# Two accumulators of one tile read by VectorE at a block's end, and a buffer of its own for the last block's gate product

## The chip, the cores and the metric

The program runs on one core of a Trainium2 chip. The metric is device time in microseconds (us), the median of several executions. The core has five engines with an instruction queue each: TensorE (PE in the profile; PEld are its weight loads), VectorE (DVE), ScalarE (ACT), GpSimd (POOL) and SyncE (SP), which here only issues transfers. TensorE adds its products up in the accumulation memory (PSUM); the other tiles lie in the on-chip memory (SBUF).

## The reference

Attention of two kinds on 4 x 8 heads of 576 positions, then two layers on the 2304 tokens. The change lies in the first layer and at its hand-over to the second.

```python
x = attention(q, k, v)            # pooled by 4, plus local |i - j| < 4
x = x.transpose(0, 2, 1, 3).reshape(2304, 512)
a = x @ w_a                       # 512 -> 1536, the gate
b = x @ w_b                       # 512 -> 1536
y = a * b @ w_out                 # 1536 -> 512, the first layer's result

h = y @ w_in                      # 512 -> 1024
e = exp(h - max(h)); sm = e / (sum(e) + 1e-9)
s = h * sm
ln = (s - mean(s)) / sqrt(var(s) + 1e-6) * g_ln
out = ln @ w_out2                 # 1024 -> 512
```

## The kernel before, in words

Every fp32 operand is split into a high and a low part, and each product is made of three matmuls (high x high, high x low, low x high).

**First layer.** The tokens go through in five blocks: four of 512 columns (`WIDE`) and a last one of 256. A block runs over 12 chunks `j` of the 1536 inner columns. For a chunk, `emit_A` with n=0 makes the gate product and with n=1 the second one (12 matmuls each, into `ab`, of which there are two tiles). `emit_a` copies the gate product out of PSUM (ScalarE, L478, tile `a`), `emit_mult` multiplies it by the second product (VectorE, L483), `emit_p` splits the result into `ph` (ScalarE, L489) and `pl` (GpSimd, L490), and `emit_B` adds the chunk into four accumulators (L507, 3 matmuls each, m = 0 to 3). Tile `a` has one buffer: the copy of chunk j+1 must wait until `pl` of chunk j, its last reader, is made. In a block of 512 columns two of the accumulators are tiles of their own (`acc0`, `acc1`); the other two are halves of one tile, `accS`. In the last block of 256 columns the gate and the second product of a chunk share one `ab` tile, and the four accumulators share two tiles. Waits are kept by tile: a matmul into one half of `accS` waits for a read of its other half.

**A block's end.** `emit_B` of chunk 11 copies each accumulator out as soon as its own three matmuls are issued (ScalarE, L514, tile `o`) and stores it to DRAM (`o1d`, L515, SP). It is called one chunk late, between the products of the next block; next come 32 small matmuls of local attention (`lS`, L353) and the gate product of the next block's chunk 1.

**Beside the last block** the second layer starts. Its 16 weight pieces are loaded (`raw`, L101, 512 KB each) into the places of first-layer weights that the last block is done with, so each load waits for a product of that block. ScalarE (L109, L110, L123 or L125) and VectorE (L114, L117, L130 or L132; four pieces use GpSimd for the last step) turn a piece into its two parts. The first layer's results come back (`o1r`, L530) and are split (L536, L537), and the products `h` (L548, 24 matmuls for each of 18 token tiles) begin. Then for each tile: maximum, exponential, mean (L557 to L577), a transpose through DRAM, and the product `o` (L616).

**The order** of instructions comes from a scheduler that plays the program through with its own cost estimates. `pin` holds TensorE's order as written through the first four blocks (all engines in the first). In the last block and after, the scheduler orders every engine, TensorE too.

Of the kernel before, what the change touches and what calls it, by code (L numbers as in the profile page):

```python
# [7 lines left out]
F32 = mybir.dt.float32  # L8
# [15 lines left out]
WIDE = 512  # L24
# [3 lines left out]
NCH = FF1 // 128  # L28
# [10 lines left out]
def kernel(  # L39
# [17 lines left out]
    PE, ACT, DVE, POOL, SP = nc.tensor, nc.scalar, nc.vector, nc.gpsimd, nc.sync  # L57
# [17 lines left out]
    base = pool("base", bufs=1)  # L75
# [7 lines left out]
    width = [min(WIDE, NT - WIDE * i) for i in range(NBLK)]  # L83
    o1d = [dram.tile([w // 128, 128, 512], F32, name=f"o1d{i}") for i, w in enumerate(width)]
# [371 lines left out]
    accs = {}  # L456
    abs_ = {}
    o1s = {}
# [15 lines left out]
                          start=(k == 0 and i == 0), stop=(k == 3 and i == 2), skip_group_check=True)  # L474

    def emit_a(blk, j):
        a = base.tile([128, WIDE], F32, tag="a", name="a")[:, 0:width[blk]]
        ACT.copy(out=a, in_=abs_[blk, j][0])  # L478
        abs_[blk, j].append(a)

# [12 lines left out]
    def emit_B(blk, j):  # L493
        w = width[blk]
        if j == 0:
            if w == WIDE:
                t = aps.tile([128, 2, 512], F32, tag="S", name="accS")
                accs[blk] = [ps.tile([128, 512], F32, tag=f"acc{n}", name=f"acc{n}") for n in range(2)] + [t[:, n] for n in range(2)]
            else:
                t = [ps.tile([128, 2, 256], F32, tag=f"acc{n}", name=f"acc{n}") for n in range(2)]  # L500
                accs[blk] = [t[n // 2][:, n % 2, :] for n in range(4)]
        ph, pl = pt.pop((blk, j))
        wh, wl = W1[3 * j + 2]
        for m in range(4):
            ms = slice(m * 128, m * 128 + 128)
            for i, (wt, x) in enumerate(((wh, ph), (wh, pl), (wl, ph))):
                PE.matmul(out=accs[blk][m], lhsT=wt[:, ms], rhs=x,  # L507
                          start=(j == 0 and i == 0 and (w == WIDE or m % 2 == 0)), stop=(j == NCH - 1 and i == 2),
                          skip_group_check=True)
            if j == NCH - 1:  # L510
                if m == 0:
                    o1s[blk] = base.tile([128, NP, WIDE], F32, tag="xs", name="o1")
                o1 = o1s[blk][:, m, 0:w]
                ACT.copy(out=o1, in_=accs[blk][m])  # L514
                SP.dma_start(out=o1d[blk][:, :, 128 * m:128 * m + 128].rearrange("i p t -> p i t"),  # L515
                              in_=o1.rearrange("p (i t) -> p i t", t=128))


    p2 = {}
# [170 lines left out]
    for i in range(6, 3 * NCH):  # L690
        j = i // 3
        t = 4 * j - 6 + 1.33 * (i % 3)
# [38 lines left out]
    for blk in range(NBLK - 1):  # L731
        for j in range(NCH):
            c = NCH * blk + j
            if c == 4:
                SP.dma_start(out=g_sb, in_=g)
            if c:
                emit_A(blk, j, 0, 0, WIDE)
            emit_a(blk, j)
            if c:
                advance(4 * c + 1.33)  # L740
                emit_A(blk, j, 1, 0, WIDE)
            emit_mult(blk, j)
            if j == NCH - 1:
                advance(4 * c + 2)
                emit_p(blk, j)
                split_x(blk + 1)
                advance(4 * c + 2.67)
            else:
                advance(4 * c + 2.67)
                emit_p(blk, j)  # L750
            if prev:
                emit_B(*prev.pop())
            prev.append((blk, j))
            advance(4 * c + 4)
            pin(None if blk == 0 else (PE.engine,))
    blk = NBLK - 1
    advance(1e9)
    for j in range(NCH):
        if j == 2:
            start_p2()  # L760
        for n in range(2):
            emit_A(blk, j, n, 0, width[blk])
            (emit_mult if n else emit_a)(blk, j)
        emit_p(blk, j)
        prev.append((blk, j))
        if len(prev) > 2 or j < 1:
            emit_B(*prev.pop(0))
        if j == 8:
            split_o1(0)
            split_o1(1)  # L770
            load_o1(2)
            load_o1(3)
        for t_, f in w2q:
            if t_ == j:
                f()
    for x in prev:
        emit_B(*x)
# [92 lines left out]
```

## Time and profile before

| | |
|---|---|
| median of 3 executions | 805.21 us (800.87 to 806.71) |
| the profiled execution | 803.08 us, of which the span from the first to the last instruction is 801.3 us |
| TensorE busy in the span | 765.4 us (96%), mean granted clock 0.988 |
| VectorE, ScalarE, GpSimd busy | 376.9, 332.5, 228.5 us |

A matmul's time in the profile reaches from its start to the modelled end, and matmuls overlap, so the distance between two starts is the pace. An idle time stands in square brackets with the engine and line that ended it. Times in the trace count from the first instruction; what lies outside the span is 803.08 - 801.3 = 1.8 us.

### The profile page before, as it was taken

The page shows a single profiled execution, that of the slowest core. Times are in us where ns is not written, and L with a number is a line of the kernel's source. Part 1 is how long each engine was busy: PE and PEld are TensorE (multiplying, and loading weights), DVE is VectorE, ACT ScalarE, POOL GpSimd, SP SyncE. Part 2 cuts the span into 40 slices and gives each one's busy share as a digit, 9 for nine tenths or more (in the row PEclk, how much of TensorE's full clock was granted, in tenths as well). Part 3 has the DMA queues.
Part 4 walks back from the last instruction along what each step waited for, and adds up shares of the span by engine and source line. Part 5 has one row for each costly group of instructions (what it writes and reads, how often), then busy time and mean ns, then how long its engine had stood idle before and what let it go on. Part 6 is the DMA issues. An engine that isn't in the chain of part 4 may idle for free.

```text
span 801.3 us, 12378 instructions
## 1 busy us (share of the span) xinstructions
PE 765.4 (96%) x4848; PEld 621.3 (78%) x4848; DVE 376.9 (47%) x689; ACT 332.5 (41%) x691; POOL 228.5 (29%) x204
## 2 busy tenths in 40 slices
PE   4979999998999999999999999999899999999997
PEld 3867777776787787777787888888788888888885
DVE  5678889974223324223213220126765373545441
ACT  3648777653222324322323221147645343344432
POOL 1242343431322222232111121114222352334320
PEclk9979999999999999999999999999999999999999
DMA  8977844214212203111102000036422554444321
GB/s 239 239 259 246 268 152 137 70 30 139 59 57 61 83 30 110 59 52 34 42 15 80 15 27 1 0 112 208 155 79 66 157 173 144 145 134 145 103 79 40
DMA packets 65226, 85.04 MB, mean 106 GB/s; under 512 B 9016, under 2 KB 46136, under 8 KB 65168
## 3 DMA queue, kind: packets, MB, share of 16 engines
q1 hardware_dynamic: 64864, 84.02, 33.8%
q8 instruction: 38, 0.62, 0.3%
q10 hardware_dynamic: 304, 0.23, 0.1%
q14 instruction: 20, 0.16, 0.1%
HBM read 66.93 MB, written 17.30 MB: 105 GB/s over the span
## 4 chain that ended last, share of the span: by engine, by line
PE 81%; DVE 7%; ACT 5%; DMA 3%; issue 3%; POOL 1%; SPq 0%; DVEq 0%; ACTq 0%; POOLq 0%
PE ab L473 33%; PE o L616 13%; PE h L548 11%; PE acc L507 8%; PE accS L507 7%; PE lo L412 2%; PE pv L283 2%; PE lPT L393 2%; DVE wm L117 2%; DMA qkr<-qkp 1%; PE lS L353 1%; PE S L223 1%; DMA raw<-w 1%; PE PT L266 1%; ACT o L514 1%
## 5 line engine op out<-in xcount | busy, mean ns | idle before, releaser
L473 PE MATMUL ab<-xTh,w 128*128 128x512 f32 (+1 forms) x976 | 298.0, 375 | 6.2 <-DVE a L483 3.6
L473 PEld LDWEIGHTS ab<-xTh,w 128*128 128x128 f32 x976 | 179.9, 191 | 43.7 <-DVE a L483 5.6
L473 PE MATMUL ab<-xTl,w 128*128 128x512 f32 (+1 forms) x488 | 180.2, 369 | 0.9 <-DVE xTl L167 0.5
L490 POOL TENSOR_TENSOR pl<-a,ph 128x512 fp32r<-128x512 f32 (+1 forms) x60 | 75.1, 1251 | 234.6 <-ACT ph L489 234.6
L483 DVE TENSOR_TENSOR a<-a,ab 128x512 f32<-128x512 f32 (+1 forms) x60 | 38.0, 632 | 181.3 <-PE ab L473 181.3
L473 PEld LDWEIGHTS ab<-xTl,w 128*128 128x128 f32 x488 | 93.4, 191 | 15.1 <-DVE xTl L167 0.9
L548 PE MATMUL h<-w,o1w 128*128 128x512 f32 x432 | 103.9, 391 | 1.1 <-ACT w L123 0.9
L548 PEld LDWEIGHTS h<-w,o1w 128*128 128x128 f32 x432 | 80.1, 188 | 18.1 <-ACT w L123 1.1
L616 PE MATMUL o<-w,cTh 128*128 128x512 f32 x288 | 91.0, 397 | 1.2 <-ACT cTh L606 0.9
L507 PE MATMUL acc<-ph,w 128*128 128x512 f32 (+1 forms) x288 | 90.2, 365 | 0.0
L478 ACT COPY a<-ab 128x512 f32<-128x512 f32 (+1 forms) x60 | 32.5, 542 | 108.9 <-PE ab L473 103.7
L507 PE MATMUL accS<-ph,w 128*128 128x512 f32 x192 | 68.0, 391 | 4.2 <-ACT o L514 4.2
L616 PEld LDWEIGHTS o<-w,cTh 128*128 128x128 f32 x288 | 54.0, 188 | 14.3 <-ACT cTh L606 1.1
L489 ACT CAST ph<-a 128x512 fp32r<-128x512 f32 (+1 forms) x60 | 34.6, 577 | 67.2 <-DVE a L483 67.2
L507 PEld LDWEIGHTS acc<-ph,w 128*128 128x128 f32 x288 | 52.2, 189 | 9.1 <-issue 1.2
L616 PE MATMUL o<-w,cTl 128*128 128x512 f32 x144 | 57.2, 397 | 0.1
L507 PE MATMUL acc<-pl,w 128*128 128x512 f32 (+1 forms) x144 | 51.1, 358 | 0.1
L600 POOL TENSOR_TENSOR cTl<-raw,cTh 128x1024 fp32r<-128x1024 f32 x15 | 36.0, 2401 | 44.2 <-ACT cTh L599 36.6
L507 PEld LDWEIGHTS accS<-ph,w 128*128 128x128 f32 x192 | 36.0, 188 | 13.1 <-ACT o L514 5.5
L117 DVE CUSTOM_DVE_ANT_0 wm<-raw,wm 128x1024 uint16<-128x1024 uint16 x52 | 43.4, 845 | 2.3
L255 POOL TENSOR_TENSOR E<-E,ss 72x576 f32<-72x576 f32 x16 | 19.3, 1206 | 81.1 <-DVE ss L253 53.4
L557 DVE TENSOR_REDUCE mx<-h 128x1 f32<-128x1024 f32 x18 | 22.0, 1223 | 43.1 <-PE h L548 43.1
(91 smaller groups left out, 1005.5 us busy)
## 6 DMA issues: line engine op xcount, KB each, us to landing
raw<-w SPq DMA_DIRECT2D x52, 512.0 KB
qkr<-qkp SPq DMA_DIRECT2D x32, 288.0 KB
vd<-v SPq DMA_DIRECT2D x15, 512.0 KB
raw<-vd SPq DMA_DIRECT2D x60, 128.0 KB
vw<-vwin SPq DMA_DIRECT2D x36, 140.0 KB
vp<-vp SPq DMA_DIRECT2D x16, 288.0 KB
o1r<-o1d SPq DMA_DIRECT2D x18, 256.0 KB
out<-ob SPq DMA_DIRECT2D x18, 256.0 KB
```

The source lines that it names most:

```text
L117: DVE.tensor_tensor(out=st["w"], in0=st["w"], in1=st["low"], op=ALU.add)
L255: POOL.tensor_tensor(out=ev, in0=ev, in1=st["ss"].to_broadcast([72, 4, SD]), op=ALU.mult)
L473: PE.matmul(out=abs_[blk, j][n][:, c0:c1], lhsT=w[:, ws], rhs=x[:, k, c0:c1], start=(k == 0 and i == 0), stop=(k == 3 and i == 2), skip_gr ...
L478: ACT.copy(out=a, in_=abs_[blk, j][0])
L483: DVE.tensor_tensor(out=a, in0=a, in1=pb, op=ALU.mult)
L489: ACT.copy(out=ph, in_=a)
L490: POOL.tensor_tensor(out=pl, in0=a, in1=f32(ph), op=ALU.subtract)
L507: PE.matmul(out=accs[blk][m], lhsT=wt[:, ms], rhs=x, start=(j == 0 and i == 0 and (w == WIDE or m % 2 == 0)), stop=(j == NCH - 1 and i == ...
L548: PE.matmul(out=h[:, n * 512:n * 512 + 512], lhsT=x[:, ks], rhs=w, start=(k == 0 and q_ == 0), stop=(k == 3 and q_ == 2))
L557: DVE.tensor_reduce(out=mx, in_=st["h"], axis=AX.X, op=ALU.max)
L600: POOL.tensor_tensor(out=h4(lo), in0=raw, in1=f32(h4(hi)), op=ALU.subtract)
L616: PE.matmul(out=o, lhsT=x[:, k, :], rhs=w, start=(k == 0 and q_ == 0), stop=(k == 7 and q_ == 2))
```

## The change

In a 512-column block the copies for m = 0 and 1 stay where they are, on ScalarE. The copies for m = 2 and 3, the two halves of `accS`, move behind the last matmul of the block and from ScalarE to VectorE, and their two stores with them. In the last block the gate copy gets a tag `a2` of its own with two buffers of 256 columns.

```diff
     def emit_a(blk, j):
-        a = base.tile([128, WIDE], F32, tag="a", name="a")[:, 0:width[blk]]
+        if width[blk] == WIDE:
+            a = base.tile([128, WIDE], F32, tag="a", name="a")
+        else:
+            a = base.tile([128, 256], F32, tag="a2", bufs=2, name="a")
         ACT.copy(out=a, in_=abs_[blk, j][0])
...
+        def store(m):
+            SP.dma_start(out=o1d[blk][:, :, 128 * m:128 * m + 128].rearrange("i p t -> p i t"),
+                         in_=o1s[blk][:, m, 0:w].rearrange("p (i t) -> p i t", t=128))
...
-                o1 = o1s[blk][:, m, 0:w]
-                ACT.copy(out=o1, in_=accs[blk][m])
-                SP.dma_start(out=o1d[blk][:, :, 128 * m:128 * m + 128].rearrange("i p t -> p i t"),
-                              in_=o1.rearrange("p (i t) -> p i t", t=128))
+                if m < 2 or w < WIDE:
+                    ACT.copy(out=o1s[blk][:, m, 0:w], in_=accs[blk][m])
+                    store(m)
+        if j == NCH - 1 and w == WIDE:
+            for m in (2, 3):
+                DVE.tensor_copy(out=o1s[blk][:, m, 0:w], in_=accs[blk][m])
+                store(m)
```

Through the first four blocks the order on TensorE and GpSimd stays as it was; ScalarE loses and VectorE gains two copies at each block's end. There ScalarE has, before, at the end of the first block (`o` is the copied result, `lP` and `E` belong to attention):

```order
L514 COPY o_2079<-acc_885 128x512
L489 CAST ph<-a 128x512
L514 COPY o_2079<-acc_886 128x512
L514 COPY o_2079<-accS 128x512 x2
L374 ACTIVATE lP<-lP 128x560
```

The two `accS` copies now stand on VectorE at the same place, between the multiplication of the next block's chunk 0 and the mask of the local attention (`lP`), with the multiplication of chunk 1 further behind:

```order
L486 TENSOR_TENSOR a<-a,ab 128x512
L253 RECIPROCAL ss<-ss 72x4
L526 COPY o_2079<-accS 128x512 x2
L364 TENSOR_TENSOR lP<-lS,mk_sb 128x280 x2
L370 TENSOR_REDUCE lmx<-lP 128x8
L371 TENSOR_TENSOR lP<-lP,lmx 128x560
L380 TENSOR_REDUCE lsm<-lP 128x8
L381 TENSOR_SCALAR lsm<-lsm 128x8
L382 RECIPROCAL lsm<-lsm 128x8
L486 TENSOR_TENSOR a<-a,ab 128x512 x2
```

From the fourth block's end on every engine is in another order. The last block's start on TensorE before (`ab_4809`, `ab_4862`, `ab_4906` hold the products of chunks 0, 1, 2; `w1` is chunk 0's second product, `w6` chunk 2's gate):

```order
L473 MATMUL ab_4809<-xTh_4787,w1_562 128x256
L507 MATMUL accS_4233<-ph_4783,w35_1955 128x512
L507 MATMUL accS_4233<-pl_4784,w35_1955 128x512
L507 MATMUL accS_4233<-ph_4783,w35_1955 128x512
L473 MATMUL ab_4906<-xTh_4787,w6_825 128x256
```

The same place now; the three `accS` matmuls stand ahead of these rows, and chunk 1's second product (`w4`) comes at once, ahead of chunk 2's gate:

```order
L473 MATMUL ab_4809<-xTh_4787,w1_562 128x256
L473 MATMUL ab_4862<-xTh_4787,w4_636 128x256
L473 MATMUL ab_4862<-xTl_4788,w4_636 128x256
L473 MATMUL ab_4862<-xTh_4787,w4_636 128x256 x2
L473 MATMUL ab_4862<-xTl_4788,w4_636 128x256
```

In the middle of the last block VectorE had, before, up to the multiplication of chunk 5 (`a_5123`; `h_5551` and `h_5601` are the second layer's first two tiles, `wm` weight pieces on their way):

```order
L483 TENSOR_TENSOR a_5049<-a_5049,ab_5036 128x256
L557 TENSOR_REDUCE mx_5576<-h_5551 128x1
L114 TENSOR_SCALAR wm_5172<-raw_5108 128x512
L114 TENSOR_SCALAR wm_5232<-raw_5174 128x512
L557 TENSOR_REDUCE mx_5626<-h_5601 128x1
L558 TENSOR_SCALAR mx_5576<-mx_5576 128x1
L117 ISA wm_5172<-raw_5108,wm_5172 128x1024
L117 ISA wm_5232<-raw_5174,wm_5232 128x1024
L558 TENSOR_SCALAR mx_5626<-mx_5626 128x1
L483 TENSOR_TENSOR a_5123<-a_5123,ab_5110 128x256
```

Now one weight piece stands between the two multiplications, and the chain of the second layer's first tile comes behind chunk 9:

```order
L486 TENSOR_TENSOR a_5049<-a_5049,ab_5036 128x256
L114 TENSOR_SCALAR wm_5168<-raw_5106 128x512
L117 ISA wm_5168<-raw_5106,wm_5168 128x1024
L486 TENSOR_TENSOR a_5123<-a_5123,ab_5110 128x256
L132 SCALAR_TENSOR_TENSOR w12_5225<-wm_5168,g_sb_65,w12_5225 128x512
```

## Rows read from the trace of the kernel before

**Rows 1.** Waits of TensorE, 186 to 537 us: total, times, longest.

```profile
PE accS L507 <- ACT o L514: 4.2, 3, 2.5
```

**Rows 2.** Timeline at the first block's end: start, duration, engine, instruction, idle before.

```profile
187.46 0.39 PE L507 MATMUL accS<-ph,w 128*128 128x512 f32 x1
...
189.70 0.59 ACT L514 COPY o<-accS 128x512 f32<-128x512 f32 x1
...
190.34 0.50 PE L507 MATMUL accS<-ph,w 128*128 128x512 f32 x1 [2.49 <-ACT o L514]
...
191.23 0.98 PE L353 MATMUL lS<-lqk 64*64 64x70 f32 x32
...
195.15 0.39 PE L473 MATMUL ab<-xTl,w 128*128 128x512 f32 x1
```

**Rows 3.** The same timeline on TensorE at the second block's end.

```profile
311.15 0.39 PE L507 MATMUL accS<-ph,w 128*128 128x512 f32 x1
...
311.61 0.39 PE L507 MATMUL accS<-ph,w 128*128 128x512 f32 x1
...
313.81 0.72 PE L353 MATMUL lS<-lqk 64*64 64x70 f32 x32
...
316.17 0.39 PE L473 MATMUL ab<-xTl,w 128*128 128x512 f32 x1
```

**Rows 4.** The same timeline on TensorE at the third block's end.

```profile
431.77 0.39 PE L507 MATMUL accS<-ph,w 128*128 128x512 f32 x1
...
433.86 0.72 PE L353 MATMUL lS<-lqk 64*64 64x70 f32 x32
```

**Rows 5.** Stretches: length, busy time (instructions) of each engine, granted clock, DMA.

```profile
192.00:195.00 3.00, 3.00 (x15) 2.28 (x9) 2.28 (x4) 0.36 (x1) 0.00 (x0) 0.51 1.08 310
...
537.00:633.00 96.00, 90.42 (x576) 80.77 (x577) 58.08 (x111) 56.12 (x106) 31.13 (x29) 1.00 0.39 129
634.00:782.00 148.00, 148.00 (x641) 120.25 (x640) 72.35 (x140) 58.05 (x89) 52.90 (x37) 1.00 0.44 138
...
573.00:577.00 4.00, 1.76 (x15) 1.55 (x15) 4.00 (x8) 3.68 (x7) 1.47 (x1) 1.00 0.81 266
```

**Rows 6.** Groups of instructions: count | busy us, mean ns | idle before.

```profile
L514 ACT COPY o<-accS 128x512 f32<-128x512 f32 x8 | 4.7, 592 | 3.4 <-PE accS L507 3.4
...
L483 DVE TENSOR_TENSOR a<-a,ab 128x512 f32<-128x512 f32 x48 | 33.0, 687 | 173.7 <-PE ab L473 173.6
```

**Rows 7.** Timeline of VectorE behind the third block's end.

```profile
434.63 0.81 DVE L364 TENSOR_TENSOR lP<-lS,mk_sb 128x280 f32<-128x280 f32 x2 [3.72 <-PE lS L353]
...
440.35 0.69 DVE L483 TENSOR_TENSOR a<-a,ab 128x512 f32<-128x512 f32 x1 [1.45 <-PE ab L473]
```

**Rows 8.** Waits of TensorE, then of ScalarE, in the last block, 537 to 633 us.

```profile
PE ab L473 <- DVE a L483: 3.6, 3, 2.2
...
ACT raw L109 <- DMA raw<-w: 10.2, 10, 1.8
...
ACT a L478 <- POOL pl L490: 4.5, 5, 1.1
```

**Rows 9.** Timeline of TensorE and VectorE around the last block's longest stop.

```profile
572.24 2.77 DVE L117 CUSTOM_DVE_ANT_0 wm<-raw,wm 128x1024 uint16<-128x1024 uint16 x2
...
572.70 0.28 PE L507 MATMUL acc<-ph,w 128*128 128x256 f32 x1
...
572.94 0.28 PE L507 MATMUL acc<-ph,w 128*128 128x256 f32 x1
...
575.00 0.41 DVE L483 TENSOR_TENSOR a<-a,ab 128x256 f32<-128x256 f32 x1
...
575.46 0.39 PE L473 MATMUL ab<-xTh,w 128*128 128x256 f32 x1 [2.24 <-DVE a L483]
```

**Rows 10.** A weight load's issue, and ScalarE's first step on that piece.

```profile
536.54 0.67 SPq L101 DMA_DIRECT2D raw<-w  x1
...
542.37 0.67 ACT L109 ACTIVATE raw<-raw 128x512 f32<-128x512 f32 x1 [1.33 <-DMA raw<-w]
```

## Prediction

> **What bounds the kernel now.** TensorE does, nearly everywhere, so I read its waits first, then the places where they stand, and last the queues that would have to keep up. From the first block's end to the fourth's, TensorE waits for one thing only: three times, 4.2 us in all, for ScalarE's copy at L514 [rows 1]. The timeline shows where. The third accumulator's last matmul starts at 187.46, the fourth's first at 190.34, right after ScalarE's copy of the third has run from 189.70 to 190.29 [rows 2]. The two accumulators are halves of one tile, so the matmul into one half waits for the read of the other, and ScalarE comes late to that read because other work stands ahead of it. The reader is to see that nothing else stops TensorE there: as soon as the copy ends, it goes on. The same happens at the second and third block's end, shorter [rows 3, 4]. The fourth block's end shows no such stop: there the scheduler has put other matmuls in between.
>
> The last block is another matter. From 537 to 633 us TensorE is busy 90.42 of 96.00 us, so 5.6 us are idle [rows 5]; the longest share is 3.6 us for VectorE's multiplication, and behind that ScalarE itself waits 4.5 us until GpSimd is done with tile a [rows 8]. From 634 to 782 us TensorE is busy all 148.00 of 148.00 us [rows 5]: a microsecond won before 634 arrives at the end in full, unless the second layer's own chain runs dry. In the changed order the products h and o of later tiles alternate as before, so that chain has the same distance to cover.
>
> **Part 1: the copies at the blocks' ends.** Removed is the wait of the fourth accumulator at four ends, of which three show it. How much? From the start of the third accumulator's last matmul to the first lS matmul, four 512-column matmuls have to start. Their pace is (311.61 - 311.15) / 2 = 0.23 us [rows 3], so 0.92 us, and about 1.0 with the hand-over to the small matmuls (my estimate). Measured:
> first end 191.23 - 187.46 = 3.77 us, lost 2.77 [rows 2];
> second end 313.81 - 311.61 = 2.20, lost 1.20 [rows 3];
> third end 433.86 - 431.77 = 2.09, lost 1.09 [rows 4].
> Together 5.1 us, which is the 4.2 idle and the restarts after it. The order of the changed kernel has the six accS matmuls in a row with no wait between them, so this term goes whole.
>
> The first end costs more than its stop. The granted clock is 0.51 from 192 to 195 us, the lower of the two levels (1.2 GHz), after TensorE had stood for 2.49 us [rows 2, 5]. The same run of matmuls, from the first lS matmul to the same ab matmul behind it, takes 195.15 - 191.23 = 3.92 us there and 316.17 - 313.81 = 2.36 us at the second end [rows 2, 3]. The difference, 1.56 us, goes if the clock stays up. I take it as won, but one row speaks against being sure: from 573 to 577 us TensorE is busy 1.76 of 4.00 us and the clock stays at 1.00 [rows 5], so a stop of this size need not lower it.
>
> The Trainium skill ("TensorE: Matmul & The Clock Gate", section "HAM oscillation — how this bites in real kernels") describes lulls between groups of matmuls that send the clock down, so that the next group starts slow. By that rule the 1.56 us hang on the stop and part 1 gives 6.7 us; if the slow stretch had another cause, it gives 5.1. The first end agrees with the rule, the stretch at 573 us does not.
>
> Added are two VectorE copies per end. No row shows such a copy, so I bound it by the nearest: ScalarE's copy of the same tile, 592 ns, and VectorE's multiplication of the same width with one operand in PSUM, 687 ns [rows 6]. I take 0.65 us, nearer to the second since it is the same engine, or 1.3 us for two. Behind them in VectorE's queue wait the mask of local attention and then the multiplication of chunk 1. The mask began 0.77 us after lS (434.63 - 433.86) [rows 4, 7]; the copies can begin about when lS does and take 1.3, so the mask comes about 0.6 us later relative to TensorE. The chain behind it ends with 1.45 us of idle time before the multiplication [rows 7]. That covers 0.6 us, and the cost is nothing; without that cover it would be up to 0.6 us at each of three ends, 1.8 us. The accumulator's next matmul waits for the copies too, but two products (24 matmuls of 0.23 us, 5.5 us) stand ahead of it. The two stores move with the copies on SP's queue; in the first three blocks nobody near waits for them, at the fourth end one weight load stands behind them and is issued perhaps 1 us later. That ScalarE has two copies less per end is worth nothing beyond this, since TensorE waits for nothing else of it there.
>
> **Part 2: two buffers for the last block's gate copy.** Here the change is an order: with the buffer free, ScalarE can copy chunk 1's gate while chunk 0 is still being split, the scheduler therefore places chunk 1's second product straight behind chunk 0's, and the second layer's h matmuls, which before filled the gaps, come later. What can be won is the idle 5.6 us [rows 5] and the restarts. At the longest stop two starts lie 575.46 - 572.94 = 2.52 us apart where the pace is (572.94 - 572.70) / 2 = 0.12 us, so 2.40 is lost where 2.24 is shown as idle [rows 9], and the first matmul behind costs another 0.1. With ten stops or so of about 0.25 us extra, 5.6 becomes about 8 us: the upper bound. The longest stop's cause is visible: VectorE's multiplication at 575.00 stood behind two weight pieces (2.77 us) [rows 9] and two maxima of the second layer. In the new order one piece and no maximum stands there, so this stop of 2.4 us should go. ScalarE's 4.5 us of waiting for GpSimd [rows 8] should go too, being exactly the one buffer.
>
> What comes instead: fewer h matmuls lie between a weight's last use and the place where its replacement is needed. ScalarE already waits 10.2 us for weight loads [rows 8], and in its queue the casts to ph and the gate copies stand between those loads. So I take as won only the stops whose cause the new order touches, the three for VectorE's multiplication: 3.6 us [rows 8], and 2.40 - 2.24 = 0.16 us more for each, 4.1 us. The other 2.0 us of idle time, waits for weights and copies, I leave as they are, since the weights come no faster. The bounds are 8 us (all goes) and below nothing, since the new order could stop more than the old (third rival).
>
> **The sum.** 803.08 - 5.1 - 1.6 - 4.1 = 792.3 us for the profiled execution. That one lies 2.1 us below the median of the runs shown (805.21); the same gain of 10.8 us from the median is 794.4. I say 793, a gain of 1.4%.
>
> **Rivals.**
> First, part 2 gives nothing: the new order's waits for weights eat what the second buffer frees. For it: 10.2 us of load waits on ScalarE [rows 8], now with less filler on TensorE. Against it: the longest stop has a cause that the new order removes. Time: 803.1 - 6.7 = 796.4, from the median 798.5, about 797.5. That is within 1%.
>
> Second, the wait is handed on to VectorE: the copies hold up the multiplication at the three ends by more than the 1.45 us of slack, and TensorE stops for its ab tile, or the clock falls all the same. For it: the copies stand ahead of five attention steps in one queue. Against it: 0.6 us against 1.45. Time: 1.8 us and 1.6 us are lost again, 796 us; from the median 798.
>
> Third, slower than before. In the new order chunk 6's multiplication stands on VectorE behind a weight piece whose load overwrites chunk 6's own gate weight. That makes a loop: gate product, load, ScalarE, VectorE, multiplication, and only then the gate product of chunk 8. From issue to ScalarE's first step a load took 542.37 - 536.54 = 5.8 us [rows 10], and ScalarE's and VectorE's steps on it take about 3 more (an estimate: two times 0.67 us, and half of the 2.77 us [rows 9, 10]). TensorE has five groups of 12 matmuls and seven h matmuls in between, 60 x 0.12 + 7 x 0.23 = 8.8 us. So it is balanced on the edge. It decides if loads take twice as long when crowded: then about 5.8 us are lost for each of chunks 6, 7 and 8, 17.4 us, and part 2's gain is gone. Time: 803.1 - 6.7 + 17.4 = 814. Against it: loads were already crowded at 536 us, with the stores beside them, and later ones stand alone.
>
> That the change doesn't remove the wait can be left out: the order shows the matmuls in a row and the copies behind them.
>
> **How the numbers follow.** A measurement of this kernel can tell about 1% (8 us) from no change. Chances: forecast 0.62, first rival 0.22, second 0.08, third 0.08. The forecast's own spread, 788 to 798 us (part 2 between all and nothing, the clock term in or out), lies mostly beyond 1%; some 0.04 of it falls short. So faster by over 1%: 0.58; within 1%: the rest of the forecast and the first two rivals, 0.34; slower: 0.08. The range reaches from all of part 2 won, 803.1 - 6.7 - 8 = 788, less 1 for the runs' spread, to the second rival with the spread of the medians, 802; the third rival stays outside.
>
> **What would show it.** In the changed kernel's trace: no wait of accS for ScalarE; from the third accumulator's last matmul to lS about 1.0 us at all three ends; clock 1.00 behind the first end; VectorE's copies at 0.59 to 0.69 us and still some idle time before the multiplication of chunk 1; the second layer's steady stretch without idle time, begun 9 to 13 us earlier. Part 2 is wrong if TensorE's idle time in the last block stays above 5 us, and the whole prediction is if a wait for weights of several microseconds stands there.

## The result, and the profile after

The changed kernel took 796.97 us (median of 7 executions, 795.89 to 799.09), the kernel before 805.21 us beside it (7 executions, 800.87 to 809.25). The ratio is 0.988, 95% interval 0.9842 to 0.9917: 1.2% faster, at least 0.8 and at most 1.6%. 793 had been predicted, with 787 to 802 as the range. The same code in a later session took 790.99 us against 805.5, ratio 0.9824 (0.978 to 0.9868); the two medians of the changed kernel lie so far apart because an execution of either kernel reaches the first block's end either early or some 6 us later (the last section shows what differs), and all seven executions of the changed kernel in the first session were late and five of its six in the second early, while those of the kernel before spread over both.

The medians therefore misstate what the change does by some microseconds to either side. I read it from the trace, from the first block's end on.

TensorE's waits in the changed kernel, first from 192 to 540 us (total, times, longest), where [rows 1] had 4.2 us for ScalarE's copies, then in the last block, where [rows 8] had 3.6 for the multiplication alone:

```profile
PE ab L473 <- ACT a L481: 0.4, 1, 0.4
```

```profile
PE ab L473 <- DVE a L486: 0.8, 1, 0.8
PE h L559 <- DVE w L130: 0.5, 1, 0.5
```

The wait of accS is gone. What is left, 1.7 us, lies in the last block (the row of 0.4 as well, at 539 us). TensorE's timeline at the first block's end, which answers to [rows 2]:

```profile
196.08 0.62 PE L514 MATMUL accS<-ph,w 128*128 128x512 f32 x2
196.53 0.39 PE L514 MATMUL accS<-pl,w 128*128 128x512 f32 x1
196.76 0.39 PE L514 MATMUL accS<-ph,w 128*128 128x512 f32 x1
197.08 0.72 PE L353 MATMUL lS<-lqk 64*64 64x70 f32 x32
```

The third accumulator's last matmul and the fourth's first stand in one row now (x2), and from there to lS it is 1.00 us, where it was 3.77. At the second and third end the same two starts are 315.94 and 316.94, and 434.94 and 435.94: 1.00 each, from 2.20 and 2.09 [rows 3, 4]. The stretches that answer to [rows 5] (length, TensorE's busy time, granted clock, DMA):

```profile
192.00:195.00 3.00, 3.00 (x15) 1.00 0.53 187
537.00:633.00 96.00, 94.28 (x608) 1.00 0.49 154
573.00:577.00 4.00, 4.00 (x29) 1.00 0.62 164
```

The first row lies ahead of the end now, since this execution came late; behind the end, from 195 to 198 and from 198 to 201 us, the clock is 1.00 too. In the last block TensorE's idle time fell from 5.6 to 1.7 us. VectorE behind the first end, which answers to [rows 7]:

```profile
197.18 1.29 DVE L526 COPY o<-accS 128x512 f32<-128x512 f32 x2 [0.27 <-PE accS L514]
198.39 0.80 DVE L364 TENSOR_TENSOR lP<-lS,mk_sb 128x280 f32<-128x280 f32 x2
...
203.61 0.69 DVE L486 TENSOR_TENSOR a<-a,ab 128x512 f32<-128x512 f32 x1 [0.96 <-PE ab L473]
```

The two copies take 1.29 us, the mask follows 1.31 us behind lS, and 0.96 us of idle time are left ahead of the multiplication of chunk 1. All three ends of the changed kernel show the same 1.31 and 0.96 us; before, it was 0.77 and 1.45 us at the second and third end. ScalarE's waits in the last block, which answer to the second and third of [rows 8]: the one for GpSimd is no longer among them, and the one for weight loads is half as long (the first row is the second layer's transposed u, not a weight):

```profile
ACT cTh L610 <- DMA raw<-vd: 8.9, 3, 5.4
ACT raw L109 <- DMA raw<-w: 5.1, 5, 1.4
```

### The profile page after: what moved, and what is told of

Its sections match the earlier page's. It is cut to its first block, busy times and chain, and to the rows that moved or that the text cites. A ratio compares the mean times of both kernels' runs of the same rounds, so it can differ in the third digit from the quotient of the medians.

```text
span 797.3 us, 12390 instructions
## 1 busy us (share of the span) xinstructions
PE 769.3 (96%) x4848; PEld 627.7 (79%) x4848; DVE 384.2 (48%) x697; ACT 327.0 (41%) x683; POOL 229.7 (29%) x204
```

## The experiments

Eight kernels ran, all on one chip with the kernel before beside them. Since the first 60 us move the medians, this table cuts each profile at two matmuls that every kernel has, the third accumulator's last one at the first and at the fourth block's end. Columns: where the first of them starts, the time from it to the second (three block ends), from there to the end of the span (the last block and the second layer), the sum of these two, and the ratio of the medians with its interval. All in us, worked out from timeline rows and spans.

| kernel | first end | three ends | the rest | sum | ratio |
|---|---|---|---|---|---|
| before | 187.46 | 346.9 | 267.0 | 613.8 | 1 |
| before again | 193.72 | 346.3 | 268.4 | 614.7 | 0.9988 (0.9954 to 1.0022) |
| changed | 196.08 | 340.4 | 260.8 | 601.2 | 0.988 (0.9842 to 0.9917) |
| changed again | 187.00 | 340.4 | 260.8 | 601.2 | 0.9824 (0.978 to 0.9868) |
| copies alone | 192.37 | 340.4 | 264.1 | 604.5 | 0.9884 (0.9833 to 0.9936) |
| two buffers alone | 187.06 | 346.6 | 259.2 | 605.8 | 0.9892 (0.9842 to 0.9942) |
| copies late, on ScalarE | 192.59 | 340.4 | 259.0 | 599.4 | 0.9826 (0.9777 to 0.9874) |
| each copy three times | 186.40 | 340.4 | 259.3 | 599.7 | 0.9829 (0.9775 to 0.9884) |
| VectorE in the old place | 188.97 | 344.0 | 258.3 | 602.2 | 0.986 (0.9813 to 0.9907) |
| copies at three ends only | 185.83 | 340.4 | 258.5 | 598.9 | 0.9833 (0.9781 to 0.9885) |

**The changed kernel again**, with no edit.

> The changed kernel once more, unchanged, for a second profile and more times on this chip. If the late start of its first profile (8.6 us later at the first block's end) was chance, the third accumulator's last matmul of the first block stands anywhere between 185 and 196 us now, and the rest of the run, from there to the end, is again about 12.6 us shorter than before. If the change causes it, it is again near 196.

It came to the first end at 187.00 us, not at 196, and both stretches behind are the same to 0.1 us. So the change does not make the late start, which came in one execution of the same code and not in the other.

**The copies alone**, part 1 without part 2:

```diff
-        if width[blk] == WIDE:
-            a = base.tile([128, WIDE], F32, tag="a", name="a")
-        else:
-            a = base.tile([128, 256], F32, tag="a2", bufs=2, name="a")
+        a = base.tile([128, WIDE], F32, tag="a", name="a")[:, 0:width[blk]]
```

> Part 1 alone: VectorE's copies behind the last product at the first four blocks' ends, tile a as before. If the two parts add up as the sum says, this kernel is 6.7 us faster than before (5.1 for the three stops, 1.6 for the slow clock behind the first), ratio 0.992, and the last block keeps about 5.6 us of idle time on TensorE. If the fourth block's end gains too, as the changed kernel's trace hints (its third accumulator's last matmul to its fourth's last is 1.6 us shorter there), it is 8.2 us and 0.990. The rival, that the second part gives nothing, has this kernel as fast as the changed one, 0.988. In the trace: third accumulator's last matmul to lS 1.0 us at three ends, clock 1.00 behind the first.

The three ends give 6.5 us, as the sum says (6.7). The rest is 2.9 us shorter as well, of which the expectation's second case, the fourth end, had 1.5: the order of the last block comes out otherwise, and TensorE's waits there are these (total, times, longest), instead of 3.6 us for the multiplication:

```profile
PE ab L473 <- DVE a L483: 1.5, 3, 0.6
PE h L556 <- ACT w L123: 0.9, 1, 0.9
PE ab L473 <- ACT a L478: 0.7, 1, 0.7
PE o L624 <- ACT o L518: 0.3, 1, 0.3
```

The stop of 2.24 us [rows 9] is gone by the order alone, with one buffer. The ratio equals the first one of the changed kernel, but the sum is 3.3 us longer than the changed kernel's, so the rival, that part 2 gives nothing, doesn't stand on it.

**Two buffers alone**, part 2 without part 1; the edit is the same lines the other way round, in the kernel before.

> Part 2 alone: two buffers for the last block's gate copy, ScalarE's copies of the accumulators as before. By the sum 4.1 us faster than before, ratio 0.995, and TensorE's three waits for ScalarE's copy are still there (4.2 us in all). The rival, that all of the gain is part 1's, has this at 1.000. The clock behind the first end is a second look at the 1.6 us: about 0.5 again if the stop of 2.5 us brings it down, 1.00 if that was chance. The start: in the changed kernel's profiled run TensorE came to the first block's end 8.6 us later than before, with the same order of work up to there. If the new tile a2 (it moves other tiles in SBUF) is the cause, this kernel, which has a2, starts late as well, near 196 us, and the one with the copies alone, which has no a2, near 187; if it is chance, the two don't follow that line.

TensorE's waits from 187 to 640 us, and two stretches behind the first end (length, busy time, granted clock, DMA):

```profile
PE accS L510 <- ACT o L517: 4.0, 3, 2.3
PE ab L473 <- DVE a L486: 0.4, 1, 0.4
```

```profile
191.00:192.00 1.00, 1.00 (x33) 0.50 1.12 337
192.00:193.00 1.00, 1.00 (x10) 0.50 1.12 334
```

The stops at the ends are all there, and the clock falls to 0.50 behind the first. In the last block one wait of 0.4 us is left, and the rest of the run is 7.8 us shorter (267.0 - 259.2), nearly twice the 4.1 of the sum and close to its upper bound of 8. The start was on time with tile a2, and late in the kernel without it: the tile's place in SBUF is not the cause.

**The copies late, but on ScalarE**, the changed kernel with one word altered:

```diff
-                DVE.tensor_copy(out=o1s[blk][:, m, 0:w], in_=accs[blk][m])
+                ACT.copy(out=o1s[blk][:, m, 0:w], in_=accs[blk][m])
```

> The changed kernel with the two copies left on ScalarE, but behind the last product like VectorE's. The prediction says that the place takes the wait away and the engine is worth nothing: then the three stops are gone here too (1.0 us from the third accumulator's last matmul to lS) and the time is the changed kernel's within 0.25%. If the engine counts, ScalarE's late copies hold up the attention steps and the gate copy behind them in its queue, TensorE waits for ScalarE (ab, lS or accS) and the kernel is 1 to 4 us slower than the changed one. The last block's order also differs somewhat, which may move the time by 1 or 2 us; so the ends are read in the trace.

The three ends take 340.4 us, as with VectorE: behind the last product it makes no difference to TensorE which engine copies. The rest is 1.8 us shorter than in the changed kernel, with another order in the last block and a single wait of 0.8 us.

**VectorE in the old place**, with two buffers:

```diff
-                ACT.copy(out=o1, in_=accs[blk][m])
+                (DVE.tensor_copy if m > 1 and w == WIDE else ACT.copy)(out=o1, in_=accs[blk][m])
```

> Two buffers as in the changed kernel, and VectorE makes the two copies, but each right behind its own accumulator's product, where ScalarE's stood. If sharing the tile is what makes the wait, the fourth accumulator's first matmul still starts a product's end and a copy behind the third's last, about 1.2 to 1.3 us, at all three ends, as at the second and third end before (1.31 and 1.20 us); against the changed kernel 1.1 us is lost at each, 3.2 in all, and from the first end to the fourth it takes about 343.6 us. Only the first end's extra lateness (2.88 us before) and the slow clock behind it go. If the engine was the cause (ScalarE late because of its queue), the stops are gone or far under 1 us and it takes 340.4.

344.0 us, where 343.6 was expected of the shared tile and 340.4 of the engine. TensorE's and VectorE's timelines at the second end:

```profile
310.31 0.39 PE L510 MATMUL accS<-ph,w 128*128 128x512 f32 x1
311.48 0.50 PE L510 MATMUL accS<-ph,w 128*128 128x512 f32 x1 [0.79 <-DVE o L517]
```

```profile
310.74 0.69 DVE L517 COPY o<-accS 128x512 f32<-128x512 f32 x1 [0.73 <-PE accS L510]
312.50 0.69 DVE L517 COPY o<-accS 128x512 f32<-128x512 f32 x1 [1.07 <-PE accS L510]
```

VectorE stands idle and copies as soon as it may, and still the fourth accumulator's first matmul comes 1.17 us behind the third's last; with ScalarE it was 1.31 here and 1.20 at the third end. At the first end it comes 1.62 us behind instead of 2.88. There VectorE was not idle: its copy starts 0.91 us behind the third accumulator's last matmul (188.97), not 0.43 as at the second end (310.74 - 310.31), because the multiplication stood ahead of it:

```profile
189.19 0.68 DVE L486 TENSOR_TENSOR a<-a,ab 128x512 f32<-128x512 f32 x1
189.88 0.66 DVE L517 COPY o<-accS 128x512 f32<-128x512 f32 x1
```

That is 0.45 us more than the 1.17, and accounts for the 0.4 us by which 344.0 exceeds 343.6. With a stop of 1.23 us idle there the clock stays at 1.00 from 191 to 195 us.

**Each copy three times**, to load VectorE's queue with four more copies at each end:

```diff
+                DVE.tensor_copy(out=o1s[blk][:, m, 0:w], in_=accs[blk][m])
+                DVE.tensor_copy(out=o1s[blk][:, m, 0:w], in_=accs[blk][m])
                 DVE.tensor_copy(out=o1s[blk][:, m, 0:w], in_=accs[blk][m])
```

> The changed kernel with each of VectorE's copies made three times, so that 2.6 us more stand ahead of the mask and of the multiplication of chunk 1 at each block's end. The prediction put the cover at the idle time before that multiplication, now 0.96 us. If that is the point from which it costs (the rival of a wait handed to VectorE), the multiplication comes 1.6 us later and TensorE loses about that at each of three ends: from the first end to the fourth 345 us instead of 340.4. If the true cover is larger, as the changed kernel's trace hints (the product that needs this multiplication's result starts over 10 us behind it), the three ends lose nothing: 340.4 us. The last block's order differs and is not read here.

The three ends lose nothing, 340.4 us. VectorE at the second end:

```profile
307.38 0.69 DVE L526 COPY o<-accS 128x512 f32<-128x512 f32 x1 [1.40 <-PE accS L514]
308.10 0.69 DVE L527 COPY o<-accS 128x512 f32<-128x512 f32 x1
308.71 0.80 DVE L364 TENSOR_TENSOR lP<-lS,mk_sb 128x280 f32<-128x280 f32 x2
309.42 0.68 DVE L528 COPY o<-accS 128x512 f32<-128x512 f32 x1
...
312.50 0.68 DVE L528 COPY o<-accS 128x512 f32<-128x512 f32 x1
...
313.98 0.68 DVE L486 TENSOR_TENSOR a<-a,ab 128x512 f32<-128x512 f32 x1
```

The scheduler put the mask between the copies, and they fill VectorE's idle times. So the multiplication starts 6.60 us behind the first copy, against 6.43 in the changed kernel (317.05 to 323.48), and not 1.6 us later. The cover holds for three times the load; where it ends, this run doesn't show.

**Copies at three ends only**, with two buffers: at the fourth end ScalarE copies as before.

```diff
-                if m < 2 or w < WIDE:
+                if m < 2 or w < WIDE or blk == 3:
...
-        if j == NCH - 1 and w == WIDE:
+        if j == NCH - 1 and w == WIDE and blk < 3:
```

> Two buffers, and VectorE's copies behind the last product at the first three ends alone; at the fourth ScalarE copies as before. TensorE's order is that of the kernel with two buffers alone. If the two parts add up where they don't touch, the three ends give 6.5 us (340.4 from the first to the fourth) and the last block 7.7, as with two buffers alone (259.1 from the fourth end's third accumulator to the end of the program): 599.5 us from the first end on, 1.6 less than the changed kernel, and the fastest with the one that leaves the copies on ScalarE. If the last block gives less because TensorE reaches it earlier while the weights come no faster, it takes about 260.8, as in the changed kernel.

The order on TensorE is that of the two buffers alone, so the gains can be added up: 6.5 and 8.5 us, 598.9 from the first end on. From 186 to 630 us TensorE is never idle (length, busy time, granted clock, DMA), and ScalarE's wait for weight loads has shrunk to 1.2 us (526 to 622 us):

```profile
186.00:526.00 340.00, 340.00 (x2199) 1.00 0.17 50
526.00:610.00 84.00, 84.00 (x566) 1.00 0.51 169
610.00:630.00 20.00, 20.00 (x88) 1.00 0.38 120
```

```profile
ACT raw L109 <- DMA raw<-w: 1.2, 3, 0.6
```

By its profile it is the fastest of all, 2.3 us below the changed kernel. Its median, 790.95 us, isn't told apart from the changed kernel's 790.99.

**The kernel before, again**, with no edit.

> The kernel before once more, unchanged. Its time is that of before by definition; its profile is wanted for two things. The start: of six profiles three came to the first block's end (third accumulator's last matmul) at 187 us and three at 192 to 196, one of them the changed kernel and one with the same code at 187. If that is chance of the execution, it is again one of these, and the times of before spread as wide as those of the others. The clock: behind the first end about 0.5 again from the matmul behind the stop of about 2.5 us on, and from the first end to the end of the program 613.8 us within 0.5.

It came to the first end at 193.72 us, late like the first profile of the changed kernel, so the start falls either way in both kernels. The stop at the first end was 1.99 us idle, and the clock fell to 0.50 behind it. From the first end on it took 614.7 us, 0.9 more than the profile that was read for the prediction and so 0.4 outside what was expected: behind the last block's longest stop, which left the clock at 1.00 then [rows 5], it fell this time (length, busy time, granted clock, DMA):

```profile
579.00:581.00 2.00, 0.02 (x1) 1.00 0.84 307
581.00:583.00 2.00, 2.00 (x14) 0.86 0.58 217
583.00:585.00 2.00, 2.00 (x6) 0.50 0.58 203
```

## Why the prediction was right, and where it was off

**The stops at the ends: right.** 5.1 us were to go, and 2.77 + 1.20 + 1.09 went: 1.00 us is left at each of the three ends. The reason had two halves, the shared tile and a ScalarE that comes late. The second half holds in the main at the first end only. With an idle VectorE in the old place the second and third end still stop, 1.17 us from start to start, so there it is the shared tile and the copy's own length (ScalarE's 1.31 and 1.20 leave at most 0.14 us for lateness). At the first end 2.88 - 1.17 = 1.71 us were lateness, and VectorE in the old place took 1.26 of it away. The work that stood ahead of ScalarE's copy there shows where the lateness came from (kernel before; the copy of `accS` follows at 189.70):

```profile
187.25 0.75 DVE L200 TENSOR_REDUCE qkds<-qkr 128x144 f32<-128x576 f32 x1 [1.34 <-DMA qkr<-qkp]
187.99 0.68 DVE L483 TENSOR_TENSOR a<-a,ab 128x512 f32<-128x512 f32 x1
188.70 0.62 ACT L489 CAST ph<-a 128x512 fp32r<-128x512 f32 x1 [1.53 <-DVE a L483]
189.22 0.58 ACT L514 COPY o<-acc 128x512 f32<-128x512 f32 x1
```

A load of attention data came late, VectorE's reduction of it held up the multiplication, and the cast that needs its result held up ScalarE's queue. So this lateness differs from execution to execution: the two starts lie 2.88, 2.38 and 2.65 us apart in the three profiles with ScalarE in the old place.

**The slow clock behind the first end: right in size.** The three ends gave 346.9 - 340.4 = 6.5 us; less the 5.1 that is 1.4, against 1.6 predicted. All three profiles with a stop of 1.99 to 2.49 us there show about 0.5 behind it, all those without it or with 1.23 us show 1.00. The doubt, from the last block's stop that was not followed by a lower clock, was as much in place: the same stop, 2.18 us idle, was followed by one in the second profile of before.

The Trainium skill ("TensorE: Matmul & The Clock Gate", section "HAM oscillation — how this bites in real kernels") describes lulls between groups of matmuls that send the clock down. The lulls of its example are longer than the stops here; the first end agrees with it all the same, the last block's stop in one profile and not in the other.

**VectorE's copies: right, with a cover that was put too small.** 0.69 us each (0.65 said), the mask 0.54 us later (0.6 said), 0.49 of the 1.45 us used up. The second rival is out: TensorE waits for VectorE at none of the three ends, and four more copies per end cost nothing, since most of their time fell into VectorE's idle times.

**Part 2: right in kind, the size was off.** The step that failed is "The other 2.0 us of idle time, waits for weights and copies, I leave as they are, since the weights come no faster." Alone, the two buffers gave 7.8 us in place of 4.1, and in the kernel with three ends 8.5 (both against the first profile of before). The first rival's reason, ScalarE waiting longer for weights in the new order, went the other way: that wait fell from 10.2 us to 5.1 in the changed kernel and 1.2 in the one with three ends. And the weights do come sooner. The last block's first-layer products end earlier, and the loads that overwrite their weights are issued earlier with them. VectorE's last multiplication of that block and SP's last weight loads, in the kernel before and in the changed one:

```profile
621.68 0.42 DVE L483 TENSOR_TENSOR a<-a,ab 128x256 f32<-128x256 f32 x1 [1.10 <-PE ab L473]
585.40 7.74 SPq L101 DMA_DIRECT2D raw<-w  x2
```

```profile
597.31 0.42 DVE L486 TENSOR_TENSOR a<-a,ab 128x256 f32<-128x256 f32 x1
556.20 19.51 SPq L101 DMA_DIRECT2D raw<-w  x7
```

Counted from the third accumulator's last matmul at the fourth end, that multiplication starts after 87.3 us before and after 60.8 in the changed kernel, and the last of the 16 loads is issued by 58.8 and by 39.2 us. All profiles agree: with one buffer 85 to 89 and 56 to 60 us (three profiles), with two 58 to 64 and 37 to 41 us (seven). How much of the gain is the second buffer's own and how much the new order's isn't separated: no kernel has the new order with one buffer, or the old order with two.

In the changed kernel itself part 2 and the fourth end gave 267.0 - 260.8 = 6.2 us together. The missing 2.3 us against the kernel with three ends go with another order of the last block, which has three small stops, 1.7 us idle, where the other has none. That late copies at the fourth end cost this as such isn't shown: the two other kernels that have them, with two buffers, took 259.0 (on ScalarE) and 259.3 us (three times on VectorE) for the rest. Orders of the last block differ by 2 or 3 us for small reasons, but the buffers tell more: with one buffer the rest took 264.1 to 268.4 us in three profiles, with two buffers 258.3 to 260.8 in seven.

**The sum.** 10.8 us were predicted; 12.6 came from the first end on (613.8 - 601.2), with both profiles of the changed kernel, and 13.5 against the second profile of before (614.7). The third rival's loop cost nothing: the last stop that is left in the last block ends at 554.47 us, ahead of VectorE's seventh multiplication (chunk 6) at 573.44. The forecast's "faster by over 1%" came out at 1.2, with an interval from 0.8 that doesn't quite exclude 1; what kept it there is the first 60 us, not the change.

## What to carry to other kernels

When two accumulators share a tile, read both behind the last product of either; at that place it made no difference here which engine read. A second buffer for a short-lived tile can be worth more than the stops that its reader shows, because the order around it can then be laid so that other waits close too; here it came out near the upper bound, not at the stops. Before a wait is left as it is, ask whether the new order moves what it waits for: the weight loads came sooner because the products ahead of them did. Cut a run at instructions that every version has and compare the pieces: a gain of 12.6 us looked like 8.2 in the medians of one session and 14.5 in the next.

## What the runs showed of the hardware

**The start.** The products pv (L283) of the first 60 us run at two speeds, and the granted clock of the record doesn't tell which. The same 32 matmuls in the changed kernel's first profile and in its second (start, duration, engine, instruction):

```profile
28.45 4.11 PE L283 MATMUL pv<-PTs,vp 72*64 72x144 f32 x32
```

```profile
25.67 2.46 PE L283 MATMUL pv<-PTs,vp 72*64 72x144 f32 x32
```

The instances between 20 and 60 us, with the least, median and greatest duration in ns, in the same two profiles:

```profile
L283 PE MATMUL pv<-PTs,vp x128: 443/448/502, 20.9 to 49.6; 72*64 72x144 f32 x128
```

```profile
L283 PE MATMUL pv<-PTs,vp x117: 286/286/501, 19.7 to 38.9; 72*64 72x144 f32 x117
```

The granted clock of 28 to 33 us reads 1.00 in the first of them, and so it does from 25 to 29 us in the second, though one takes 1.7 times as long as the other. Four of ten profiles are of the long kind (both kernels among them), with the first end at 192 to 196 us, five of the short (185.8 to 187.5), and one lies between (median 369 ns, 188.97).

The durations say what the record leaves out. In the second profile the batch of 32 products ahead of the fast one was slow as well, under a granted clock of 1.00:

```profile
18.16 4.40 PE L283 MATMUL pv<-PTs,vp 72*64 72x144 f32 x32 [1.51 <-ACT PTs L272]
```

And the 32 products lo (L412) took 1.98 us where the record reads 0.50 (first profile of before, granted 0.50 from 45 to 48 us). In the changed kernel's first profile they took as long, and then 1.15 us, both under 1.00:

```profile
47.17 1.98 PE L412 MATMUL lo<-lPTs,vw 70*64 70x64 f32 x32
```

```profile
55.32 1.97 PE L412 MATMUL lo<-lPTs,vw 70*64 70x64 f32 x32
62.92 1.15 PE L412 MATMUL lo<-lPTs,vw 70*64 70x64 f32 x32
```

So by its durations TensorE starts at the lower level in all ten profiles, while the record reads 1.00. The first rise comes between 23 and 28 us in the short kind and the one between, and between 57 and 62 us in the long kind. What decides when it comes stays open. A granted clock of 1.00 alone is no proof of speed: compare the durations of the same matmul.

**The clock behind a stop.** Of five stops of 1.99 to 2.49 us idle at the first end and in the last block four were followed by a clock of about 0.5, one wasn't, and the two of the last block stood at the same place of the same program. The length of the stop doesn't settle it: the stop of 1.23 us at the first end, with VectorE in the old place, was not followed by a fall, while this one, of 1.45 us in the first profile of before, was (granted 0.74 from 57 to 60 us):

```profile
56.71 0.39 PE L473 MATMUL ab<-xTh,w 128*128 128x256 f32 x1 [1.45 <-ACT xTh L441]
```
